# A Fourier-mixing and low-rank MLP kernel: the first batch's turn in rows, U on VectorE, filter blocks shared with ScalarE and GpSimd, stage-1 stores on SyncE, batch 1 inside the MLP

## The chip, the cores and the metric

The kernel runs on one core of a Trainium2 chip. The metric is the device time of one execution in microseconds. The kernel before took 625.9 us (median of three runs, 624.27 to 625.94). The profiled execution of it has a span of 621.1 us.

## The reference

For each of 8 batches of x (3136 tokens, 256 channels, float32) a filter is applied in the frequency domain along the tokens, then a low-rank mix over the tokens, then an MLP over the channels:

```
X = rfft(x, axis=1)                    # 1569 frequencies
y = irfft(X * (filt_r + 1j*filt_i), n=3136, axis=1)
h = (y.T @ U @ V).T                    # U: 3136 x 32, V: 32 x 3136, per batch
u = y + h
out = u + relu(u @ w_ch1) @ w_ch2      # 256 -> 1024 -> 256
```

## The kernel before

**Stages.** 3136 is 64 x 49, so the transforms are matmuls with constant matrices in two factors, in float16.
- Stage 1 (`st1`, L236): for each of the 49 residues r a matmul over 64 tokens (two residues side by side in 128 partitions, the last alone). It gives real and imaginary parts of 32 frequencies, which are evicted to `asb` (`al` for the last) and stored to `ct1` in HBM (L253, L262), a batch in 13 units.
- Stage 2 (`stage2`, L330): reads `ct1` back turned, as blocks `a2` of 98 rows (49 residues, two parts) and 4 x 256 columns (`load_a2`, L301), and transforms along r into a pair of PSUM banks, `pz`. Eight blocks a batch.
- The filter: `pz` times the filter tables. `ta` takes the whole block times `fa`, `tb` its two halves crossed over, times `fc` (L591, L593, L596, on VectorE); GpSimd adds them to `y` (L598).
- Stage 3 (`stage3`, L315): transforms back along r, evicts to `esb` (L309) and stores to `ct2` in HBM (L312).
- `low_rank` (L385): 32 matmuls of `esb` with the transformed U (`uh`) give U's product, evicted as `hp`; a matmul with `kr` (L394) adds up four parts to `h1`.
- Stage 4 (`stage4`, L429): `e2`, 8 residues of `ct2` (L408) with `h1` under them (`put_h`, L414), times `sv`, which holds the last inverse factor above V. The result `ut` is u, turned, for 512 tokens, evicted in two halves (L456 VectorE, L454 ScalarE).
- MLP: `mm1` (L458) is u times a slice of w_ch1, with ReLU on ScalarE into an `h` tile (L465); `mm2_part` (L473) is h times w_ch2 (L494) with u added by a matmul with the identity (L470); the output goes through `och` (L502) to HBM.

**Order.** The order of every engine's instructions is written out by hand: program order is queue order on each engine, and an instruction that waits holds up all behind it in its queue. DMA issues stand in the queue of the engine that starts them (SyncE, ScalarE or GpSimd). The MLP runs over groups of 512 tokens, six a batch, with a group of 128 tokens (the last residue of two batches) after every second batch. A group is eight steps; a step does `mm1` for a slice t of the group and `mm2_part` of the group before it. Work of the next batches is hung on the steps by a planner: `early[s]` runs ahead of step s's `mm1`, `plan[s]` at its end. `plan_mid` (L570) places stages 2 and 3, one VectorE multiply per step, `plan_st1` (L637) the units of stage 1, `plan_rest` (L623) the low-rank part and the loads for stage 4. `ok_dve` (L548) says which steps may take a multiply.

**Batch 0** is done ahead of the MLP and does not go through `ct1`: `u_hat` (L218) transforms U (products L229 on VectorE, sums L233 on GpSimd); `turned` (L271) does stage 1 with x as the weights, so that channels stand in the partitions, and copies the result to `fc` with the rows of one frequency next to each other (L287, L294, L296: elements 98 apart on the write side); `mid_first` (L340) turns four frequencies at a time by transposes (L344, evicted by L347 to `a2`), then does stage 2 into two bank pairs in turn, the filter with doubled matrices (L373 on VectorE, for every third block L368 and L370 on ScalarE and GpSimd) and stage 3. Then come `low_rank`, the loads for stage 4, two stage-4 matmul sets, and all of stage 1 of batch 1, and only then the first step of the MLP. `make_fa` (L562) rewrites the filter tables from batch 0's form to that of the others, in the first four steps.

**Tiles.** [...] mm1 0 and 1, mm2 2 and 3, stage 1 and stage 4 share bank 4, `pz` 5 and 6, stage 3 and low rank 7. `asb` has 2 buffers, `a2` 3, `ta` and `tb` 2, `h` 17. The filters, x, U, V and the weights are loaded by GpSimd's queue; `fb` (the filters) is cleared on VectorE first, and a load into a cleared region waits for that.

Of the kernel before, what the change touches and what calls it, by code (L numbers as in the profile page):

```python
# [13 lines left out]
MULT = mybir.AluOpType.mult  # L14
# [10 lines left out]
def _consts():  # L25
# [30 lines left out]
    w2[1, 1::2, 89:113] = -np.sin(p32)  # L56
    w2s = np.concatenate([w2[:, :, 64:128], w2[:, :, 0:64]], axis=2)
# [43 lines left out]
def kernel(  # L101
# [37 lines left out]
    def bank(tag):  # L139
        of = {"m": (0, 1), "o": (2, 3), "w": (4,), "e": (7,), "f": (0, 1, 2, 3, 4, 7), "e0": (7, 4)}[tag]  # L140
        turn[tag] = turn.get(tag, -1) + 1
        return psum[:, of[turn[tag] % len(of)], :]

# [41 lines left out]
    nc.vector.memset(fb[32:64], 0.0)  # L185
    nc.vector.memset(fb[96:128], 0.0)
    usb = sb.tile([64, NR * RANK], F16, tag="och", bufs=3, name="usb")
# [19 lines left out]
    vnat = sb.tile([128, SEQ], F16, tag="och", bufs=3, name="vnat")  # L207
    nc.gpsimd.dma_start(vnat[64:96, :], moe_V)
# [9 lines left out]
    def u_hat():  # L218
        ud = sb.tile([64, RANK, 2, NR], F16, tag="och", bufs=3, name="ud")
        nc.vector.tensor_copy(ud, free(usb, 0, 64, 0, [[1, RANK], [0, 2], [RANK, NR]]))  # L220
        for p in range(0, RANK, 8):
# [5 lines left out]
            t = [sb.tile([98, NK, 8], F32, tag=tag, bufs=2, name="ut") for tag in ("ta", "tb")]  # L227
# [5 lines left out]
            nc.gpsimd.tensor_add(uh[:, :, p:p + 8], t[0], t[1])  # L233


    def st1(b):  # L236
        for c in range(3):
            asb = sb.tile([128, 8, DM], F16, tag="asb", bufs=2, name="asb")
            for j in range(4):
                pf = bank("w" if b > 1 else "f")  # L240
# [11 lines left out]
            for h in range(2):  # L252
                nc.scalar.dma_start(dram(ct1[b], (24 * h + 8 * c) * 64 * DM,  # L253
                                         [[DM, 64], [64 * DM, 8], [1, DM]]), asb[64 * h:64 * h + 64])
            if b + 1 < NB and c:
                load_x(b + 1, c - 1)
            yield
        pf = bank("w" if b > 1 else "f")
# [3 lines left out]
        nc.scalar.dma_start(dram(ct1[b], 48 * 64 * DM, [[DM, 64], [1, DM]]), al)  # L262
        if b + 1 < NB:
            load_x(b + 1, 2)
            load_x(b + 1, 3)
# [5 lines left out]
    def turned(c):  # L271
        n = 8 if c < 3 else 1
        for hh in range(2):
            for g in range(0, n, 4):
                z = bank("f")
                for i in range(min(n, 4)):
                    if c < 3:
# [4 lines left out]
                    else:  # L282
                        nc.tensor.matmul(z[:, 0:64], xt[0, 3][:, 128 * hh:128 * hh + 128],
# [426 lines left out]
```

## Time and profile before

| | before |
|---|---|
| time, median of 3 | 625.9 us |
| span of the profiled execution | 621.1 us |
| TensorE matmul busy | 514.4 us (83%), 4467 matmuls |
| ScalarE busy | 397.6 us (64%) |
| VectorE busy | 360.9 us (58%) |
| GpSimd busy | 174.0 us (28%) |
| HBM read, written | 57.42 MB, 49.77 MB |
| first matmul of the MLP (L462) | at 98.15 us |
| TensorE busy in 0 to 100 us, by tens | 0.00, 4.69, 0.44, 3.81, 4.49, 8.62, 7.74, 1.90, 6.26, 1.85 |

A group line of the page names line, engine, operation, the tile written and those read, its shape and count; then busy time and mean duration, then the idle time of the engine just before these instructions and what ended it. PE is TensorE's matmul, PEld its weight load, DVE VectorE, ACT ScalarE, POOL GpSimd, SP SyncE; a q after an engine's name is its queue, where a DMA is issued or a wait ends. The chain of waits is followed back from the last instruction, at each step to what released it. The timeline lists instructions by their start, in us from the start of the span. Matmul busy time counts a matmul's whole way through the array, so a busy TensorE is not one at its peak.

### The profile page before, as it was taken

Reading aid. Unit: us, or ns where it says so; the run is one execution under the profiler, and the core shown is the slowest. Engines: PE = TensorE matmul, PEld = TensorE weight load, DVE = VectorE, ACT = ScalarE, POOL = GpSimd, SP = SyncE. Lnnn points to the kernel's source line nnn. Section 1 sums busy time; section 2 is a strip of 40 time slices with the busy share of each in tenths; the row PEclk is TensorE's granted clock in tenths of the full one; section 3 lists DMA queues with packets and bytes.
Section 4 is the critical chain, followed back from the end, with each engine's and each line's share of the span. In section 5 each row is a group of like instructions: output and inputs, shape, how many; then the busy total and the mean of one; then the engine's idle time right before and its main releaser. Section 6 shows DMA issues by size and latency. Waiting matters only on the chain.

```text
span 621.1 us, 11266 instructions
## 1 busy us (share of the span) xinstructions
PE 514.4 (83%) x4467; PEld 376.3 (61%) x4467; DVE 360.9 (58%) x372; ACT 397.6 (64%) x719; POOL 174.0 (28%) x129
## 2 busy tenths in 40 slices
PE   2128545898899889999999889998989889999997
PEld 1124222666567667667767566666767657777775
DVE  7195227777667628773875547764776369832222
ACT  0358515677577656776676658775676757776663
POOL 6814710434133302431231303340422123310000
PEclk9999867999899999999999899999999999999999
DMA  9971485369656584696548775697364454443212
GB/s 214 148 141 38 110 159 154 112 160 239 169 169 166 142 207 126 186 227 165 172 137 222 160 181 153 163 227 194 101 192 142 113 167 137 137 141 111 97 63 98
DMA packets 82597, 95.31 MB, mean 153 GB/s; under 512 B 6853, under 2 KB 63640, under 8 KB 82544
## 3 DMA queue, kind: packets, MB, share of 16 engines
q1 hardware_dynamic: 52000, 67.16, 36.1%
q0 software_dynamic: 7360, 15.91, 15.5%
q10 hardware_dynamic: 23184, 11.53, 7.1%
q8 instruction: 35, 0.57, 0.4%
q14 instruction: 18, 0.15, 0.1%
HBM read 57.42 MB, written 49.77 MB: 173 GB/s over the span
## 4 chain that ended last, share of the span: by engine, by line
PE 58%; DVE 9%; ACT 8%; DMA 8%; ACTq 4%; issue 4%; SPq 1%; POOL 1%; DVEq 0%; POOLq 0%
PE psum L494 21%; PE psum L462 20%; ACTq L253 4%; PE psum L335 4%; DMA a<-ct 4%; PE psum L327 3%; PE psum L448 3%; ACT asb L249 3%; PE psum L470 3%; ACT h L465 2%; DVE tb L596 2%; DVE tb L593 2%; ACT esb L309 2%; PE psum L242 2%; DMA ct<-asb 1%
## 5 line engine op out<-in xcount | busy, mean ns | idle before, releaser
L465 ACT ACTIVATE h<-psum 128x512 f16<-128x512 f32 (+1 forms) x416 | 238.2, 577 | 136.5 <-PE psum L462 110.8
L462 PE MATMUL psum<-ut,w1sb 128*128 128x512 f16 (+1 forms) x832 | 241.9, 374 | 19.1 <-ACT al L261 9.9
L494 PE MATMUL psum<-w2sb,h 128*128 128x256 f16 x1536 | 232.0, 274 | 0.0
L598 POOL TENSOR_TENSOR y<-ta,tb 128x1024 f16<-128x1024 f16 x56 | 118.9, 2122 | 330.1 <-DVE tb L596 294.8
L494 PEld LDWEIGHTS <-h 128*128 128x128 f16 x1536 | 143.8, 98 | 62.2 <-issue 2.6
L462 PEld LDWEIGHTS <-w1sb 128*128 128x128 f16 x832 | 104.5, 145 | 47.3 <-issue 32.5
L502 DVE COPY och<-psum 128x512 f32<-128x512 f32 x96 | 66.2, 689 | 90.8 <-PE psum L470 90.2
L591 DVE TENSOR_TENSOR ta<-psum,fb 128x1024 f16<-128x1024 f32 x56 | 68.6, 1225 | 41.1 <-PE psum L335 37.8
L309 ACT CAST esb<-psum 98x512 f16<-98x512 f32 x128 | 74.9, 590 | 10.4 <-PE psum L327 7.9
L456 DVE CAST ut<-psum 128x512 f16<-128x512 f32 x48 | 35.4, 738 | 74.9 <-PE psum L448 53.9
L593 DVE SCALAR_TENSOR_TENSOR tb<-psum,fc 64x1024 f16<-64x1024 f32 x56 | 68.7, 1226 | 1.4
L596 DVE TENSOR_TENSOR tb<-psum,fc 64x1024 f16<-64x1024 f32 x56 | 68.2, 1218 | 1.0
L335 PE MATMUL psum<-a,w2t 98*128 98x512 f16 x135 | 41.5, 386 | 18.5 <-DVE tb L596 8.3
L448 PEld LDWEIGHTS <-e 96*128 96x128 f16 x768 | 36.2, 99 | 33.7 <-issue 16.2
L249 ACT CAST asb<-psum 128x512 f16<-128x512 f32 x78 | 45.6, 587 | 16.4 <-PE psum L242 8.8
L470 PE MATMUL psum<-idn,ut 128*128 128x128 f16 x392 | 54.2, 220 | 0.0
L448 PE MATMUL psum<-sv,e 96*128 96x64 f16 x768 | 39.2, 195 | 14.1 <-issue 8.2
L327 PE MATMUL psum<-y,g 128*98 128x512 f16 x105 | 39.8, 379 | 6.9 <-ACT esb L309 6.4
L454 ACT CAST ut<-psum 128x512 f16<-128x512 f32 x48 | 35.4, 737 | 9.9 <-PE psum L448 9.9
L470 PEld LDWEIGHTS <-ut 128*128 128x128 f16 x392 | 38.5, 98 | 5.0
L242 PE MATMUL psum<-x,wf 128*128 128x256 f16 x168 | 32.8, 292 | 1.1 <-ACT asb L249 1.1
L296 ACT CAST fc<-psum 128x256 f16<-128x256 f32 x12 | 14.9, 1687 | 21.0 <-PE psum L278 21.0
(76 smaller groups left out, 266.8 us busy)
## 6 DMA issues: line engine op xcount, KB each, us to landing
out_dram<-och SPq DMA_DIRECT2D x48, 512.0 KB
ct<-esb SPq DMA_DIRECT2D x64, 196.0 KB
x<-in_x_dram POOLq DMA_DIRECT2D x24, 512.0 KB, 8.0
e<-ct SPq DMA_DIRECT2D x48, 256.0 KB
a<-ct SPq DMA_DIRECT2D x56, 196.0 KB
ct<-asb ACTq DMA_DIRECT2D x42, 256.0 KB
e<-h SPq DMA_DIRECT2D x24, 128.0 KB
wf<-wf SPq DMA_DIRECT2D x3, 256.0 KB
```

The source lines that it names most:

```text
L309: nc.scalar.copy(esb[b, k][:, 2 * half:2 * half + 2, :].rearrange("p s d -> p (s d)"), pe[0:98])
L335: nc.tensor.matmul(pz, w, a, start=True, stop=True)
L448: nc.tensor.matmul(pu[:, 64 * i:64 * i + 64], e2[b, c][:, i, 128 * dh:128 * dh + 128], sv[:, 64 * r:64 * r + 64], start=(i == 0), stop=Tru ...
L462: nc.tensor.matmul(ph[:, 0:n], w1sb[:, dh, :, t], gr.ut[:, dh, 0:n], start=(dh == 0), stop=(dh == 1))
L465: nc.scalar.activation(h[:, 0:n], ph[:, 0:n], RELU)
L470: nc.tensor.matmul(o[:, dh * 128:dh * 128 + 128], gr.ut[:, dh, t0:t0 + n], idn, start=False, stop=(dh == 1), skip_group_check=True)
L494: nc.tensor.matmul(o, gr.h[tt][:, i * 128:(i + 1) * 128], w2sb[:, tt, :], start=(tt == 0), stop=False, skip_group_check=True)
L502: nc.vector.tensor_copy(gr.och[:, 2 * y:2 * y + 2, :].rearrange("p j d -> p (j d)"), gr.pc)
L591: nc.vector.tensor_mul(ta, pz, va)
L593: nc.vector.scalar_tensor_tensor(out=tb[0:64], in0=pz[64:128], scalar=-1.0, in1=vb, op0=MULT, op1=MULT)
L596: nc.vector.tensor_mul(tb[64:128], pz[0:64], vb)
L598: nc.gpsimd.tensor_add(ys[k], ta, tb)
```

## The change

It is one rewrite with several parts:
- The turn of batch 0: `turned` copies PSUM to `fc` in one piece, 512 elements in a row, and the transposes read columns 32 apart. For this the rows of the stage-2 matrix, and the order of the rows in `ct1`, change.
- `u_hat`: U's copy is divided between VectorE and ScalarE, and the sums go from GpSimd to VectorE. One half of the clearing of `fb` is done by a ScalarE copy from a small cleared tile.
- The middle of batch 0: the evictions of the transposes go from ScalarE to VectorE, and 6 instead of 5 of 16 filter blocks go through ScalarE and GpSimd. x of batch 1 is loaded from inside it.
- The filter blocks of the other batches: two of eight (three in batch 1) are copied out of PSUM by ScalarE, and GpSimd does all their multiplies. The minus sign moves from the multiply into the table (`make_fa`), so that L593 becomes a plain multiply.
- Stage-1 stores are issued by SyncE, not ScalarE, and `asb` has three buffers.
- Stage 1 of batch 1 moves from before the MLP into its steps 3 to 7, three units a step; x of batch 2 is loaded from steps 9 to 15. An empty group of eight half-steps after batch 0 gives batch 1 time to get ready.
- Both halves of `ut` are evicted by VectorE; steps 2 and 6 take no multiply. The second low-rank matmul comes a step later. Three `a2` loads are ahead instead of two, stage 3 comes a step later. U, V and the h tiles share one ring.

```diff
+    order = np.append(np.arange(48).reshape(2, 24).T.reshape(-1), 48)
+    w2 = w2.reshape(2, NR, 2, 128)[:, order].reshape(2, 98, 128)
...
-        of = {..., "e0": (7, 4)}[tag]
+        of = {..., "e0": (7, 4), "w1": (7, 5, 6)}[tag]
...
+    NH = 17
+    hring = cst.tile([128, NH, 512], F16, name="hring")
+    hflat = hring.rearrange("p n f -> p (n f)")
...
-    nc.vector.memset(fb[32:64], 0.0)
+    zero = cst.tile([128, 64], F16, name="zero")
+    nc.vector.memset(zero, 0.0)
     nc.vector.memset(fb[96:128], 0.0)
-    usb = sb.tile([64, NR * RANK], F16, tag="och", bufs=3, name="usb")
+    nc.scalar.copy(fb[32:64].rearrange("p s (k f) -> p (s k) f", f=64),
+                   free(zero, 32, 64, 0, [[0, NK * DM // 64], [1, 64]]))
+    usb = hflat[0:64, 0:NR * RANK]
...
-        nc.vector.tensor_copy(ud, free(usb, 0, 64, 0, [[1, RANK], [0, 2], [RANK, NR]]))
+        for p, eng in ((0, nc.vector.tensor_copy), (16, nc.scalar.copy)):
+            eng(ud[:, p:p + 16], ...)
...
-            nc.gpsimd.tensor_add(uh[:, :, p:p + 8], t[0], t[1])
+            nc.vector.tensor_add(uh[:, :, p:p + 8], t[0], t[1])
...
-            asb = sb.tile([128, 8, DM], F16, tag="asb", bufs=2, name="asb")
+            asb = sb.tile([128, 8, DM], F16, tag="asb", bufs=3, name="asb")
-                pf = bank("w" if b > 1 else "f")
+                pf = bank("w" if b > 1 else "w1")
...
-                nc.scalar.dma_start(dram(ct1[b], (24 * h + 8 * c) * 64 * DM,
-                                         [[DM, 64], [64 * DM, 8], [1, DM]]), asb[64 * h:64 * h + 64])
+                nc.sync.dma_start(dram(ct1[b], (16 * c + h) * 64 * DM,
+                                       [[DM, 64], [128 * DM, 8], [1, DM]]), asb[64 * h:64 * h + 64])
...
-                    dst = free(fc, 0, 128, 3136 * hh + 2 * (24 * h + 8 * c + g),
-                               [[2, 4], [1, 2], [98, 32]])
+                if hh:
+                    nc.vector.tensor_copy(cm[:, o:o + n], z[:, 0:n])
+                else:
+                    nc.scalar.copy(cm[:, o:o + n], z[:, 0:n])
...
-                                        free(fc, 0, 128, 3136 * hh + 98 * (4 * k + i), [[1, 98]]), idn)
-            a2[k] = sb.tile([98, 4 * DM], F16, tag="a2", bufs=3, name="a2")
-            nc.scalar.copy(a2[k], z[0:98])
+                                        free(fc, 0, 128, 3136 * hh + 4 * k + i, [[32, 98]]), idn)
+            a2[k] = sb.tile([98, 4 * DM], F16, tag="a2", bufs=4, name="a2")
+            nc.vector.tensor_copy(a2[k], z[0:98])
...
-            if j % 3 == 2:
+            if j % 5 in (1, 3):
...
+            if j in (4, 6, 8, 10):
+                load_x(1, j // 2 - 2)
...
+        if b == 0:
+            groups.append(Group(None, 7))
...
-        if dh:
-            nc.scalar.copy(o, v)
-        else:
-            nc.vector.tensor_copy(o, v)
+        nc.vector.tensor_copy(o, v)
...
-    for _ in st1(1):
-        pass
...
-        return s % 8 != 2 and not small(s)
+        return s % 8 not in (2, 6) and not small(s)
...
-        nc.vector.tensor_copy(fc[64:128, s], fb[64:128, s])
+        nc.vector.tensor_copy(fc[0:64, s], fb[64:128, s])
+        nc.vector.tensor_scalar_mul(fc[64:128, s], fb[64:128, s], -1.0)
         nc.vector.tensor_copy(fa[64:128, s], fb[0:64, s])
...
-                nc.vector.scalar_tensor_tensor(out=tb[0:64], in0=pz[64:128], scalar=-1.0, in1=vb,
-                                               op0=MULT, op1=MULT)
+                eng.tensor_mul(tb[0:64], p[64:128], vb[64:128])
...
+        def pooled(k):
+            pc = sb.tile([128, 4 * DM], F16, tag="pc", bufs=2, name="pc")
+            nc.scalar.copy(pc, box[k][0])
+            box[k][0] = pc
+            for i in range(3):
+                mul(k, i, nc.gpsimd)
...
+        lead = 5 if b > 1 else 2
+        for k in range(3):
+            at(later(s, -lead), fetch, k)
...
+            if k in on_pool:
+                s = later(s, 1)
+                early[s].append((pooled, (k,)))
+                d = max(later(s, 10), end)
+                s = later(s, 3 if b > 1 else 1)
+            else:
...
+                d = max(later(s, 5), end)
+                s = later(s, 1)
+            at(d, three, k, 0)
+            at(later(d, 1), three, k, 1)
...
+        at(later(s, 2), low_rank_end, b)
...
+    for u in range(13):
+        at(3 + u // 3, step1, 1)
+    for c in range(4):
+        at(9 + 2 * c, load_x, 2, c)
...
-        m = later(start[b - 1], -8) if b > 1 else 5
-        z = plan_mid(b, m, 0 if b == 1 else 3)
+        m = later(start[b - 1], -8) if b > 1 else 10
+        z = plan_mid(b, m, (2, 5) if b > 1 else (1, 3, 5))
```

## The prediction

> **What bounds the kernel now.** I read the busy table by slices first (TensorE fills its slices from about 110 us on, and does little in the first 98), then the chain of waits from 0 to 125 us, the timeline of the first 50 us, and TensorE's waits in the regular part. The chain through the start:
>
> ```profile
> 71.27 2.30 DMA ct<-esb
> ...
> 73.63 3.49 DMA e<-ct
> 77.12 3.73 issue
> 80.85 0.60 PE psum L448 x8
> ...
> 86.12 8.82 DMA ct<-asb
> ...
> 98.15 2.72 PE psum L462 x6
> ```
>
> The first matmul of the MLP (L462) starts at 98.15. Ahead of it stands a round trip through memory (71.27 to 80.85), and then all of batch 1's stage 1 (82.91 to 98.15), most of it one wait of 8.82 us for a store, because only two asb buffers exist. What stands before 71 is in the timeline of the first 50 us (start, length, engine, line; idle time and releaser in brackets):
>
> ```profile
> 27.63 1.44 POOL L233 TENSOR_TENSOR uh<-ut 98x256 f16<-98x256 f32 x2
> 28.43 2.00 DVE L229 TENSOR_TENSOR ut<-psum,tw 98x256 f32<-98x256 f32 x4 [13.14 <-POOL uh L233]
> ...
> 30.18 9.95 ACT L296 CAST fc<-psum 128x256 f16<-128x256 f32 x8 [9.40 <-PE psum L278]
> 30.28 14.74 DVE L294 CAST fc<-psum 128x256 f16<-128x256 f32 x12
> ```
>
> The lines of L229 and L233 are the products and additions of U, L296 and L294 the turned copies of batch 0. VectorE stood 13.14 us because the additions of U (L233) are queued on GpSimd behind all filter loads, which that queue finishes issuing at 27.63. Only then come the turned copies, 14.74 / 12 = 1.23 us each for 256 scattered elements. In the regular part TensorE's waits between 182 and 560 us (us, times, longest) are:
>
> ```profile
> PE psum L462 <- ACT h L465: 8.8, 12, 1.1
> PE psum L335 <- DVE tb L596: 6.8, 8, 1.2
> PE psum L335 <- DMA a<-ct: 6.6, 5, 2.0
> PE psum L327 <- ACT esb L309: 5.2, 3, 1.8
> PE psum L394 <- ACT hp L392: 2.8, 6, 0.5
> ```
>
> That is 30.2 us of 378: TensorE is the bound here, and only these waits can go. The chain around 180 us shows what makes ScalarE late: it issues stores itself.
>
> ```profile
> 179.39 0.59 ACT asb L249
> ...
> 180.01 0.62 ACTq L253
> ...
> 180.66 0.90 ACTq L253
> ```
>
> For 1.5 us no ReLU can run behind an L249, so the next matmul of L462 comes late.
>
> [...] 577 ns for 512 and 1017 for 1024 elements, so 0.86 ns each and 0.14 us fixed. [...] the trace has 2122 ns (L598). [...] the multiply L591 has a minimum, median and maximum of 1224, 1225 and 1225 ns, and GpSimd runs beside some of them. So more GpSimd work shouldn't slow these multiplies. [...] The windows show a granted clock of 0.63 and 0.54 in 80 to 100 us, after the idle stretch; I leave as much of that in the new start.
>
> **U and the turn.** VectorE clears one half of fb instead of two (3.47 us less). The other half goes to ScalarE: 8192 elements x 0.86 + 0.14 = 7.2 us, after its table load (1.28), so from about 2.0 to 9.2. GpSimd's second filter load waits for it, where it waited for VectorE until 9.80 before: no change. The loads of su and tw queue behind it on ScalarE; su leaves at about 9.7 and lands 1.9 us later (the smallest load in the page's list of landings needs that), 11.6. The copy of U in halves (2.78 us before, 1.4 to 1.6 each now) ends at 12.8 on ScalarE. VectorE starts the U products at about 12.5: four rounds of two multiplies (618 ns each) and one addition. The addition isn't in the trace on VectorE; it lies between 0.25 (256 elements at the 0.89 ns of L220) and 0.74 (GpSimd's own), and I take 0.4. That makes 4 x 1.64 = 6.6, to 19.1. The turned copies become six of 128x512 in a row per engine: VectorE 6 x 0.69 (L247) + 0.2 = 4.3, to 23.4; ScalarE 6 x 0.58, hidden beside it. x has landed by 18.1, where the filter issues stop waiting for it. So the transposes start near 23.5 and not 45.47: -22 (-25 to -18). Their weights are read with a stride of 32 elements; w1sb's with a stride of 8 take 145 instead of 98 ns. 64 of these would cost 3 us on a TensorE that isn't this stage's bound: 0 to 2.
>
> **The middle of batch 0** lasts from 45.47 to 71.25, 25.8 us; its busiest engine is ScalarE with 13 x 1.02 + 16 x 0.54 = 21.9. Now VectorE has 10 multiplies x 1.225 and 8 copies of 98x1024 (1.02 to 1.3, I take 1.15) = 21.5, ScalarE 14.8, GpSimd 6 x 2.12. With the same 3.9 us of filling and handing over: 25.4, taken as 26 with the strided weights (24 to 28). It ends near 49.5. The last filter load is issued at 25.34 and lands at 27.2; the last quarter is needed 18 us after 23.5. Hidden. The loads of x for batch 1 stand on GpSimd between its multiplies, half a microsecond each, and have 20 us to land.
>
> **The tail** to the first L462 is 71.25 to 83.05 without stage 1 of batch 1: 11.8. The load of x for batch 2 (at 76.45) no longer runs beside it: 11.4. The MLP starts at 49.5 + 11.4 = 60.9 instead of 98.15: **-37.2**.
>
> **The first groups get it back in part.** VectorE now has 12 x 0.69 = 8.3 us of filter copies (8 before; the negated one is priced like L564), then 6 evictions of stage 1 x 0.69 and two ut copies x 0.74: about 14. Behind them wait stage 1's matmuls, in order with the MLP's, so group 0 takes 14 to 15 instead of 7.3: +7. The last store (2.3 to 3 us) and the a2 load (3.3) follow it, against three steps of slack of 1.2 each: a wait of about 3 where 0.9 and 1.7 were: +0.5. The empty group of eight half-steps splits 7.9 us of MLP into 4.4 of only mm2 and about 6 of only mm1, bound by ScalarE's ReLUs (8 x 0.6): +2. Gone are ScalarE's store issues in the rest of this part (waits of 1.9 and 1.8 at 122 and 134): -3.2. Sum: **+6.3** (+2 to +12).
>
> **The regular part.** Off ScalarE per batch: six ut copies x 0.737 and seven store issues x 0.6; onto it two copies x 1.02. VectorE loses 2 x 3.67 of multiplies and gains 4.4. Both stay under 50 us of a 62 us batch. Waits: L462 8.8 to 2; L394 2.8 to 0 (its matmul comes a step later); L335 on DMA 6.6 to 2 (three loads, ahead of the e loads on SyncE); L335 on VectorE 6.8 to 3 (a pooled block frees its banks after 1.02 instead of 3.67); L327 5.2 to 3. That is -20.2. New: a pooled block needs 1.02 on ScalarE, up to 2.1 behind an addition, and 4 x 2.12 = 8.5 on GpSimd, 11.6 of the 12.5 us that ten steps give; its y may come late, behind it queue stage 3 and the MLP: +3. The stores now stand on SyncE behind output stores and e loads; three asb buffers hide that. The new order of ct1's rows (w2's rows permuted to match) moves the same packets, and U, V and the 17 h tiles in one ring only change place, since U and V are read before the first ReLU writes there: both 0. Sum: **-17.2** (-28 to 0).
>
> 625.9 - 37.2 + 6.3 - 17.2 = 577.8, so **577**.
>
> **Rivals.** (1) The start gains, the regular part does not: each wait of ScalarE comes back as one of SyncE's order or GpSimd's y. For it: the 0.9 us of slack above. Against: GpSimd is busy 28% only. 625.9 - 37.2 + 6.3 = 595. (2) All waits of the regular part go, and the first group overlaps better: -39 + 2 - 28 = 561. Against: the small groups still have too short steps for VectorE. (3) Slower: [...] Then a pooled block needs 12.7 and its wait 3 us more, the next block's addition queues behind, 4 us for each of 15 blocks: +60, and the gain in waits shrinks to 8: 625.9 - 37.2 + 6.3 + 60 - 8 = 647.
>
> **How the numbers follow.** 0.55 for my forecast, 0.22 for (1), 0.16 for (2), 0.06 for (3), 0.01 for no change. The range takes in the bounds of the start (about 6 either way) and reaches to (1) and near to (2): 557 to 600. Faster 0.93, same 0.01, slower 0.06.
>
> **What would show it.** First L344 near 23.5, first L475 near 61 in the new lines; group 0 near 14 us; no ACTq store in the chain; L335 and L475 waits as above. Wrong: U's products starting after 15, a middle of batch 0 over 29, GpSimd multiplies of 64x1024 over 2.2 us, or stage 3 waiting for GpSimd's y in each batch.

## The result, and the profile after

The changed kernel takes **608.98 us** (median of four runs, 601.8 to 610.12) where the kernel before takes 625.92 beside it: a ratio of 0.970, with a 95% interval of 0.961 to 0.978. It is faster, but by 17 us and not by the 48 that were forecast, and 609 lies outside the range of 557 to 600. Its profiled execution has a span of 599.7 us and is the shortest of the four; the other three have spans of 607.0 to 608.1.

I divided both profiled executions into three stretches: up to the first matmul of the MLP (L462, now L471), from there to the first step of the second group of batch 1, and the rest. The last column is the median over the runs of the changed kernel and of its variants in which nothing of that stretch was edited (6, 5 and 8 profiles, this one among them; for the first groups the run with x of batch 2 held back counts too).

| | before | forecast | after, profiled | after, median |
|---|---|---|---|---|
| start, to the first mm1 of the MLP | 98.2 | 60.9 | 65.5 | 66.1 |
| first groups | 81.0 | 87.3 | 101.5 | 102.6 |
| regular part | 441.9 | 424.7 | 432.6 | 437.0 |
| span | 621.1 | 572.9 | 599.7 | 605.7 |

So the start is 5 us worse than forecast, the first groups 15 and the regular part 12, in the typical run. The profile of the kernel before is of an execution of 622.9 us, 3 us under its median, so the last column set against the first shows up to 3 us too little gain. The timeline of the changed kernel's start:

```profile
9.07 2.86 ACT L231 COPY hring<-hring 64x1568 f16<-64x1568 f16 x1
10.00 1.09 DVE L241 TENSOR_TENSOR ut<-psum,tw 98x256 f32<-98x256 f32 x2 [0.96 <-PE psum L236]
11.12 0.42 DVE L245 TENSOR_TENSOR uh<-ut 98x256 f16<-98x256 f32 x1
...
15.82 2.48 DVE L299 CAST fc<-psum 128x512 f16<-128x512 f32 x4
...
52.85 1.74 SPq L418 DMA_DIRECT2D e<-ct  x3
...
54.34 0.61 POOL L165 DMA_DIRECT2D x<-in_x_dram  x1
55.27 2.94 SPq L424 DMA_DIRECT2D e<-h  x3
```

U's products (L241) begin at 10.00 and no longer wait for GpSimd. In the kernel before the first half of them ran at 13.28, as this line of its timeline shows, and the other half only at 28.43:

```profile
13.28 2.01 DVE L229 TENSOR_TENSOR ut<-psum,tw 98x256 f32<-98x256 f32 x4 [0.96 <-PE psum L224]
```

The turned copies (L299) take 0.62 us apiece. The last three lines of the first view are the new tail: three e loads, then a load of x for batch 2 issued right into them, then the puts of h. TensorE's waits in the regular part (167 to 560 us; us, times, longest):

```profile
PE psum L340 <- DMA a<-ct: 10.5, 4, 3.0
PE psum L340 <- DVE tb L600: 4.4, 9, 1.1
PE psum L460 <- DMA a<-ct: 3.1, 1, 3.1
PE psum L332 <- ACT esb L314: 0.9, 3, 0.4
```

The 8.8 us in which mm1 waited for its ReLU and the 2.8 us of the low-rank end are gone from the list, stage 3's 5.2 us are 0.9. The waits for a2 have grown from 6.6 us to 10.5 and 3.1 (the second is a matmul of stage 4, whose wait the profile puts down to the same transfers). The first two groups, in windows (length; busy time and instructions of each engine; granted clock; share of the DMA engines; GB/s):

```profile
core 0: us, PE busy (x) PEld busy (x) DVE busy (x) ACT busy (x) POOL busy (x), PEclk, DMA share, GB/s
65.50:83.60 18.10, 11.31 (x62) 6.38 (x59) 14.53 (x24) 7.38 (x14) 0.95 (x1) 0.71 0.36 70
83.60:100.30 16.70, 11.17 (x80) 7.38 (x80) 6.16 (x8) 5.86 (x11) 1.68 (x1) 0.80 0.50 129
```

They take 34.8 us where the first two took 19.4 before. TensorE waits in both, and once more ahead of batch 1's first group. Its longest waits from 65 to 167 us:

```profile
PE psum L254 <- DVE asb L259: 6.3, 1, 6.3
PE psum L340 <- DMA a<-ct: 5.9, 2, 5.5
PE psum L460 <- DMA e<-h: 5.4, 1, 5.4
```

The first ends at 77.6 (stage 1 of batch 1, for its eviction on VectorE), the second at 92.3 (stage 2, for the a2 data), the third at 151.8 (stage 4 of batch 1, for the put of h). The mean clock of the two groups is 0.71 and 0.80: the trace has it at half (0.50) from 75.9 to 82.7 and from 89.5 to 96.3, and later from 150.9 to 157.8.

### The profile page after: what moved, and what is told of

It is laid out like the page before. It is cut to its first block, busy times and chain, and to the rows that moved or that the text cites. A ratio compares the mean times of both kernels' runs of the same rounds, so it can differ in the third digit from the quotient of the medians.

```text
span 599.7 us, 11562 instructions
## 1 busy us (share of the span) xinstructions
PE 525.0 (88%) x4467; PEld 383.4 (64%) x4467; DVE 332.2 (55%) x384; ACT 379.8 (63%) x676; POOL 266.5 (44%) x171
## 3 DMA queue, kind: packets, MB, share of 16 engines
q0 software_dynamic: 7360, 15.91, 16.3%
## 4 chain that ended last, share of the span: by engine, by line
PE 54%; DVE 8%; ACT 3%; DMA 3%; issue 2%; SPq 2%; DVEq 0%; ACTq 0%
PE psum L471 19%; PE psum L504 19%; PE psum L340 3%; PE psum L460 3%; PE psum L480 3%; PE psum L332 3%; DVE tb L600 2%; DVE tb L598 2%; DMA a<-ct 2%; PE psum L254 2%; DVE och L512 1%; DVE ta L596 1%; PE psum L396 1%; ACT asb L261 1%; SPq L424 1%
## 5 line engine op out<-in xcount | busy, mean ns | idle before, releaser
L475 ACT ACTIVATE hring<-psum 128x512 f16<-128x512 f32 (+1 forms) x416 | 238.2, 576 | 160.7 <-PE psum L471 158.7
L471 PE MATMUL psum<-ut,w1sb 128*128 128x512 f16 (+1 forms) x832 | 243.6, 375 | 0.5 <-DVE ut L465 0.4
L504 PE MATMUL psum<-w2sb,hring 128*128 128x256 f16 x1536 | 233.7, 276 | 0.0
L504 PEld LDWEIGHTS <-hring 128*128 128x128 f16 x1536 | 145.1, 99 | 62.3 <-issue 1.9
L465 DVE CAST ut<-psum 128x512 f16<-128x512 f32 x96 | 71.0, 740 | 150.0 <-PE psum L460 135.5
L471 PEld LDWEIGHTS <-w1sb 128*128 128x128 f16 x832 | 103.2, 145 | 22.7 <-issue 6.2
L596 DVE TENSOR_TENSOR ta<-psum,fb 128x1024 f16<-128x1024 f32 x41 | 50.1, 1221 | 35.3 <-PE psum L340 32.0
L340 PE MATMUL psum<-a,w2t 98*128 98x512 f16 x135 | 43.0, 400 | 22.9 <-DMA a<-ct 16.5
L598 DVE TENSOR_TENSOR tb<-psum,fc 64x1024 f16<-64x1024 f32 x41 | 50.2, 1226 | 1.0
L600 DVE TENSOR_TENSOR tb<-psum,fc 64x1024 f16<-64x1024 f32 x41 | 49.9, 1217 | 0.6
L332 PE MATMUL psum<-y,g 128*98 128x512 f16 x105 | 39.8, 379 | 2.7 <-ACT esb L314 1.5
L340 PEld LDWEIGHTS <-w2t 98*128 98x128 f16 x135 | 13.7, 102 | 31.5 <-issue 26.5
L598 POOL TENSOR_TENSOR tb<-pc,fc 64x1024 f16<-64x1024 f16 x15 | 31.9, 2123 | 1.2
```

The costliest lines, as they stand in the source:

```text
L340: nc.tensor.matmul(pz, w, a, start=True, stop=True)
L465: nc.vector.tensor_copy(o, v)
L471: nc.tensor.matmul(ph[:, 0:n], w1sb[:, dh, :, t], gr.ut[:, dh, 0:n], start=(dh == 0), stop=(dh == 1))
L475: nc.scalar.activation(h[:, 0:n], ph[:, 0:n], RELU)
L504: nc.tensor.matmul(o, gr.h[tt][:, i * 128:(i + 1) * 128], w2sb[:, tt, :], start=(tt == 0), stop=False, skip_group_check=True)
L598: eng.tensor_mul(tb[0:64], p[64:128], vb[64:128])
```

## The experiments

All times are medians, compared with the changed kernel's 609.0 unless another is named; the kernel before took 625.9 to 627.2 beside each of them. Intervals are those of the ratio to the kernel before. Where nothing ahead of the MLP is edited, its first matmul still lies between 65.1 and 69.0 us in six profiles, so a difference of 2 to 3 us in the start of a single profile tells nothing.

### The tail: x of batch 2 held back

```diff
+    def hold():
+        nc.gpsimd.tensor_copy(gate, groups[0].ut[0:1, 1, 510:512])
+    at(9, hold)
     for c in range(4):
         at(9 + 2 * c, load_x, 2, c)
```

> The changed kernel, with the four loads of x(2) held on GpSimd's queue until the second ut copy of group 0 exists (a copy of two elements on GpSimd reads it ahead of them), so that none is issued at 54.3 us. Theory A: the x(2,0) load, 8.35 us on its way beside the e loads and the put of h, is what makes the tail after the middle of batch 0 15.5 us and not 11.4; then e<-h lands 3 to 4.5 us after its issue instead of 6.1, MLP begins at 61 to 63 instead of 65.55, and the kernel takes 2.5 to 4 us less, with no wait on x(2) anywhere. Rival B: e<-h stands behind the e loads, which are alone enough to take that long; then MLP begins within 1 us of 65.5 and the time is the same within 1 us.

603.65 us (0.964, 0.958 to 0.970): 5.3 less. The MLP begins at 62.3; the puts of h land 3.8 to 3.9 us after their issue instead of 6.1 to 7.6. Theory A holds, and the gain is above its 4 us. One of the four x buffers is free by then, and the change took the load out of stage 1, so nothing on GpSimd's queue held it until the tail was over.

### The first groups

Three runs: `make_fa` spread over the groups, `make_fa` in the tail, stage 1 of batch 1 in the tail.

```diff
-        at(i, make_fa, i)
+        at((8, 14, 21, 28)[i], make_fa, i)
```

> The changed kernel, with its four make_fa calls after steps 8, 14, 21 and 28 instead of after steps 0 to 3 (each is first read at step 11, 17, 24 or 31). Theory A: in group 0 the stage-1 evictions of batch 1 on VectorE (L259) stand behind the 10.3 us chain of L570 to L572 from 66.5 to 76.8, which is the 6.5 us gap of TensorE at 77.6 and brings the half-clock stretch with it. Then group 0 falls from 18.1 us to 10 to 12, the L254 wait on L259 from 6.3 us to under 1, and the kernel takes 5 to 9 us less than the changed one (about 601 to 604 median). Rival B: group 0 is held by its 31 stage-1 pieces on TensorE and ScalarE whatever VectorE does, and the wait moves to the a2 fetch of group 1; then group 0 and 1 together stay at 33 to 35 us and the time within 2 us of the changed kernel.

612.79 us (0.977, 0.970 to 0.983): 3.8 more. Group 0 falls to 10.7 us, as theory A says, so the chain of L570 to L572 was what held stage 1's evictions. In group 1 the wait for the a2 data grows from 5.5 to 7.7 us, as rival B had it. And groups 1 to 3 take 19.2, 18.6 and 17.9 us instead of 16.7, 11.3 and 11.4, which neither theory had. VectorE's groups of lines, first of this run from 76 to 135 us (busy time, mean ns, idle time before):

```profile
L572 DVE COPY fb<-fb 64x2048 f16<-64x2048 f16 x4 | 8.0, 2009 | 0.3
L571 DVE TENSOR_SCALAR fc<-fb 64x2048 f16<-64x2048 f16 x4 | 6.7, 1686 | 0.1
L570 DVE COPY fc<-fb 64x2048 f16<-64x2048 f16 x4 | 5.2, 1291 | 0.1
```

and of the changed kernel from 65 to 123 us:

```profile
L571 DVE TENSOR_SCALAR fc<-fb 64x2048 f16<-64x2048 f16 x4 | 2.8, 692 | 0.1
L570 DVE COPY fc<-fb 64x2048 f16<-64x2048 f16 x4 | 2.8, 688 | 0.1
L572 DVE COPY fb<-fb 64x2048 f16<-64x2048 f16 x4 | 2.7, 686 | 0.4
```

The same twelve instructions take 19.9 us where they took 8.3, while GpSimd now multiplies beside them (17.2 of 18.6 us busy in group 2); the next run shows one such copy at 7.37 us beside a GpSimd copy. Behind them the ut copy is late, and stage 1 of batch 2, which shares its bank, waits 10.3 us for it.

```diff
+    for i in range(4):
+        make_fa(i)
+    stage4(groups[0], 0)
```

> The changed kernel, with the four make_fa calls on VectorE between the middle of batch 0 and the first ut copy, where VectorE is idle from 47.6 to 64.4 us, instead of in group 0. Theory A (from the run with make_fa spread): these f16 copies take 0.69 us alone and 1.7 to 2.8 us beside GpSimd's work; in the tail the first three or four run beside the sv copy (2 to 2.8 us), the rest alone, in all 10 to 16 us, so the chain ends between 58 and 64, at most 1 us after what stage 4 waits for. Group 0 falls to 10 to 12 us, group 1 stays at 15 to 19 (its a2 fetch comes no earlier relative to stage 1), and the kernel takes 4 to 8 us less than the changed one. Rival B: the sv copy on GpSimd is slowed by VectorE's copies as much as they by it (6.9 to 10 us or more), stage 4 waits for sv, MLP begins 2 to 4 us later, and the gain is under 4 us.

602.6 us (0.960, 0.953 to 0.968): 6.4 less, theory A. MLP begins at 67.2, group 0 is 10.3 us, group 1 stays at 19.0. The timeline of VectorE and GpSimd in this tail:

```profile
48.36 6.91 POOL L524 COPY sv<-hring 32x3136 f16<-32x3136 f16 x1
48.46 7.37 DVE L568 COPY fc<-fb 64x2048 f16<-64x2048 f16 x1
55.84 0.69 DVE L569 TENSOR_SCALAR fc<-fb 64x2048 f16<-64x2048 f16 x1
```

VectorE's copy, begun 0.1 us after GpSimd's, ends 0.56 us after it, at 55.83; GpSimd's takes 6.91 us, and 6.90 in the changed kernel, where no VectorE copy runs beside it. The expectation had assumed slower copies; here only the first one is long, and the next ones take 0.69 us each. Rival B, that the sv copy is slowed, is refuted.

```diff
+    for _ in st1(1):
+        pass
     stage4(groups[0], 0)
...
-    for u in range(13):
-        at(3 + u // 3, step1, 1)
```

> The changed kernel, with stage 1 of batch 1 issued as a whole between the low-rank products of batch 0 and its first stage 4 (where TensorE is idle from 51.3 to 63.6 us, ScalarE from 51.5) instead of at steps 3 to 7 of group 0: this undoes the part that put batch 1 into MLP. Theory A: it fits into the idle time but for its stores, which share the DMA engines with the e loads and the put of h; MLP begins 0 to 3 us later (65.5 to 68.5), group 0 takes 8.5 to 11 us instead of 18.1 and group 1 10 to 12 instead of 16.7, since the a2 data are long there; the kernel takes 8 to 13 us less. Rival B: the 1.6 MB of stores hold up the put of h and MLP begins 5 us or more later, and groups 2 to 5 inherit the waits; gain under 5 us.

600.43 us (0.960, 0.953 to 0.968): 8.6 less, theory A. MLP begins at 67.9 (2.3 later), group 0 takes 7.2 us. Group 1 takes 15.7 and not 10 to 12: in it mm1 waits 4.5 us for a ut copy that stands behind `make_fa`, which now falls wholly into this time. The first groups last 90.2 us instead of 102.6.

### The middle of batch 0

```diff
-                                        free(fc, 0, 128, 3136 * hh + 4 * k + i, [[32, 98]]), idn)
+                                        free(fc, 0, 128, 3136 * hh + 98 * (4 * k + i), [[1, 98]]), idn)
```

> The changed kernel, with the 64 transposes of batch 0 reading 98 neighbouring columns at 98*(4k+i) instead of 98 columns with a stride of 32; batch 0's input to stage 2 is wrong by this (the columns are in another order), everything else is computed as before. Theory A: the strided weight loads are what made eight transposes take 1.3 to 1.48 us instead of 0.45 to 0.61, and TensorE the bound of batch 0's middle. Then they take 0.45 to 0.65, the middle of batch 0 (20.4 to 49.97, 29.6 us) takes 23 to 26, MLP begins 3 to 6 us earlier, and the kernel takes 3 to 6 us less. Rival B: the middle is bound by the VectorE chain of a2 copies and products, and the transposes wait for their bank; then the eight still take over 1.2 us and the middle stays at 29 to 30.

This kernel leaves out the order of columns that its contiguous copies need, so batch 0's values don't count, only its time. One run: 608.95 us. The transposes of the changed kernel, by source line (minimum, median, maximum in ns, first and last start):

```profile
L349 PEld LDWEIGHTS <-fc x64: 241/261/273, 20.4 to 42.0; 128*98 128x98 f16 x64
L349 PE MATMUL psum<-idn,fc x64: 220/332/428, 20.4 to 42.1; 128*98 128x128 f16 x64
```

and of this run:

```profile
L349 PEld LDWEIGHTS <-fc x64: 120/125/208, 19.8 to 42.1; 128*98 128x98 f16 x64
L349 PE MATMUL psum<-idn,fc x64: 217/220/315, 19.8 to 42.1; 128*98 128x128 f16 x64
```

The stride costs 136 ns a weight load, 8.7 us for 64, and the eight transposes of a block take 0.6 to 1.1 us instead of 1.4 to 1.9: that part of theory A holds. But the middle, from the first transpose to the first low-rank matmul, takes 29.7 us as against 28.9, so its conclusion fails, and so does rival B's, that the transposes would stay slow. TensorE's waits from 20 to 50 us in this run name something else, and GpSimd's timeline shows it:

```profile
PE psum L332 <- POOL uv L375: 5.6, 2, 5.3
```

```profile
29.07 0.55 POOL L220 DMA_DIRECT2D w2sb<-in_moe_w_ch_dram  x1
29.63 4.21 POOL L375 TENSOR_TENSOR uv<-pc,fb 128x1024 f16<-128x1024 f16 x2
```

GpSimd goes on issuing loads until 29.6, and only then comes to its first two products, for which ScalarE's copies have been there since 24.5 and 26.2. The next run, with batch 0's columns out of order in the same way, takes those two away from GpSimd:

```diff
-            if j % 5 in (1, 3):
+            if j in (6, 8, 11, 13):
...
-                uv = sb.tile([128, 2, 2 * DM], F16, tag="ta", bufs=3, name="uv")
+                uv = sb.tile([128, 2, 2 * DM], F16, tag="uv", bufs=5, name="uv")
```

> The run with contiguous transposes (batch 0's data wrong in the order of columns), with GpSimd's products of batch 0 reduced from six to four, j = 6, 8, 11 and 13, so that none stands behind GpSimd's own queue of loads; the two others go to VectorE, with buffers enough for them. Theory A: what kept the middle of batch 0 at 30 us with cheap transposes is that queue, which ends at 28.6 to 29.6, and the two products behind it (to 33.8, with a wait of L332 of 5.3 us); then the middle takes 21 to 25 us (bound by VectorE's 12 products of 1.23 and 8 copies of 0.69 us, 20.3 us in sum), the wait of L332 on L375 falls under 1.5 us, and MLP begins 5 to 8 us earlier than in the changed kernel. Rival B: another bound, such as the filter loads still under way, holds it at 27 us or more.

One run: 606.07 us. The middle takes 23.8 us, the wait of L332 on GpSimd 0.9, as theory A has it; MLP begins at 62.0, 3.5 earlier and not 5 to 8 (the tail is as slow as before). So two bounds of about the same length stood beside each other, TensorE with strided weights and GpSimd's queue, and taking one away leaves the other. That GpSimd's queue is one, these two runs show. That the strided weights are one by themselves rests on the trace: in the changed kernel's middle TensorE stands idle for 1.3 of 28.9 us. No run had strided weights and the two products moved. The last run of these undoes the part with contiguous copies, with the columns of batch 0 in their order:

```diff
+                for h in range(2):
+                    dst = free(fc, 0, 128, 3136 * hh + 4 * (8 * c + g) + 2 * h,
+                               [[4, 4], [1, 2], [98, 32]])
```

> The changed kernel, with batch 0's turn done as in the kernel before: the evictions of stage 1 scatter (1.23 us for 128x256 on either engine, 24 of them and two small ones, where the changed kernel has 14 copies of 0.59 to 0.69 us), and the 64 transposes read 98 neighbouring columns. This undoes the part with contiguous copies and nothing else. Theory A: copies cost 7 to 8 us more before the first transpose (27 to 29 instead of 20.4), the transposes give 6 to 9 us back on TensorE, and by then the queue of loads on GpSimd (to 28.6) no longer stands before its first product, so the middle of batch 0 takes 22 to 25 us; MLP begins within 2.5 us of the changed kernel's 65.5 and the time is within 2 us of it: the contiguous copies bring next to nothing. Rival B: the middle still takes 28 us or more, being bound by VectorE's and GpSimd's products; then 6 to 8 us slower.

612.58 us (0.976, 0.968 to 0.983): 3.6 more. Scattered copies run from 15.8 to 30.6, the first transpose is at 31.0 and not at 20.4, and the middle takes 23.1 us. So the contiguous copies gain 10.6 us and give 5.8 back in the middle. MLP begins at 70.5, 4.9 later. Rival B is refuted; theory A had the middle right and put the end of the copies 2 to 4 us too early, so its conclusion that they bring next to nothing fails.

### The regular part

```diff
-            plan_st1(b, later(start[b - 1], -55))
+            plan_st1(b, later(start[b - 1], -60))
```

> The changed kernel, with stage 1 of batches 3 to 7 begun 60 units of time before the first group of the batch ahead instead of 55. Theory A: at each batch border the first a2 fetch stands in SyncE's queue behind the last stage-1 store and waits for it to land (6.6 us after its issue at 206.5), and stage 2 waits 2 to 3 us for the fetch; with 5 units more (5 to 6 us) the store has landed when the fetch comes up. Then the waits of L340 on a<-ct from batch 3 on fall from about 2.1 to 3.2 us each to under 0.5 and the kernel takes 7 to 11 us less. Rival B: the transfers at the border are bound by the DMA engines (share 1.0 to 1.1 there), so a store issued earlier makes others late; then the waits move to stage 4 or to other borders, and the time falls by 0 to 3 us.

593.05 us (0.946, 0.941 to 0.952): 15.9 less, more than theory A's 11. The groups at the borders of batches 3 to 6, which took 15.3, 13.0, 14.2 and 13.9 us, take 11.9, 11.3, 10.2 and 11.5. It moves stage 1, its x loads and what stands in SyncE's queue together, so it doesn't tell which of them counts.

The clock has a share that theory A left out. In `gate_x2`, where this part of the kernel is as in the changed one, TensorE waits 3.3, 2.8, 3.1 and 3.3 us at the four borders, and just behind the end of each the clock goes to half for 3.4 us (from 218.9, 280.3, 348.6 and 413.5). The changed kernel's own profile, the fastest of its four executions, has two such stretches (348.9 and 413.8). With early stage 1 there is none. The border group of batch 4, first in `gate_x2`, then in this run:

```profile
276.30:290.80 14.50, 11.20 (x83) 7.55 (x82) 7.14 (x8) 5.52 (x10) 2.12 (x1) 0.88 0.70 186
278.80:290.10 11.30, 9.70 (x84) 7.08 (x83) 7.11 (x8) 6.22 (x12) 2.13 (x1) 1.00 0.78 205
```

Four stretches of 3.4 us at half the clock are up to 7 us lost (my estimate), beside the waits' own 12.5.

The border of batch 4 in the changed kernel, as SyncE's timeline and then the chain have it:

```profile
276.73 0.48 SPq L418 DMA_DIRECT2D e<-ct  x1
277.26 0.59 SPq L418 DMA_DIRECT2D e2l<-ct  x1
277.95 0.65 SPq L424 DMA_DIRECT2D e<-h  x1
278.65 0.61 SPq L424 DMA_DIRECT2D e2l<-h  x1
279.30 1.43 SPq L308 DMA_DIRECT2D a<-ct  x3
```

```profile
278.65 0.61 SPq L424
279.30 2.81 DMA a<-ct
282.15 0.59 PE psum L340 x2
```

The a2 fetches stand behind the e loads of the batch ahead, and the first of those waits for the last ct2 store. SyncE's waits of this kind from 182 to 560 us:

```profile
SPq L418 <- DMA ct<-esb: 20.9, 7, 5.0
```

The next run changes only that order:

```diff
-        lead = 5 if b > 1 else 2
+        lead = 9 if b > 1 else 2
```

> The changed kernel, with the first three a2 fetches of batches 2 to 7 planned 9 units ahead of stage 2 instead of 5, stage 1 left at -55. Theory A (queue order): at four of the five borders the fetches stand in SyncE's queue behind the first e load of the batch ahead, which waits 4 to 5 us for the last ct2 store to land; 4 units earlier they are ahead of it. Then the waits at 282, 348 and 413 us go, the groups there fall from 13.0, 14.2 and 13.9 to 10.3 to 11.3, only the border of batch 3 (where the fetch waits 4.3 us for the last stage-1 store itself) keeps its wait, and the kernel takes 6 to 10 us less. Theory B (transfer load): what counts is that the stage-1 stores, the x loads and the ct2 stores are on their way together; then the fetches only wait in place of the e loads, the waits stay at 2 to 3 us or move to stage 4, and the time falls by 0 to 3 us.

601.66 us (0.958, 0.951 to 0.965): 7.3 less, about half of what early stage 1 brings. TensorE's waits from 172 to 560 us in this run, and one of SyncE's from 182 on:

```profile
PE psum L460 <- DMA e<-h: 6.2, 4, 4.5
PE psum L340 <- DVE tb L600: 4.9, 10, 1.1
PE psum L340 <- DMA a<-ct: 3.3, 1, 3.3
```

```profile
SPq L308 <- DMA ct<-al: 17.7, 4, 7.3
```

At the borders of batches 4 to 6 the wait is gone (10.8, 10.7, 10.3 us); one wait for a2 is left, at the border of batch 3, and that one is worse (20.0 us instead of 15.3): there the fetch waits for the last stage-1 store itself, and now the e loads stand behind it. Theory A holds for its three borders, with its reverse side: whichever of the two loads waits, the other is queued behind.

The same edit in the kernel before:

```diff
-                plan_st1(b, later(start[b - 1], -52))
+                plan_st1(b, later(start[b - 1], -57))
```

> The kernel before, with stage 1 of batches 3 to 7 begun at -57 instead of -52, nothing else. Theory A: the border waits (L335 on a<-ct, 6.6 us in five) are there for the same reason and go: 4 to 8 us less than the kernel before. Theory B: in the kernel before ScalarE issues the stage-1 stores and the fetches are two with lead 5 and 4, so the border is not the same; the waits of mm1 on its ReLU stay, and the time falls by 0 to 3 us.

614.17 us (0.979, 0.974 to 0.985): 13 less than the kernel before, more than theory A's 8. Its regular part falls from 441.9 to 430.2. Two of TensorE's waits from 182 to 560 us:

```profile
PE psum L335 <- DMA a<-ct: 3.8, 5, 1.2
PE psum L462 <- ACT h L465: 3.3, 7, 0.8
```

The border waits fall from 6.6 us only to 3.8, which is the smaller part. The waits of mm1 on its ReLU fall from 8.8 to 3.3, which neither theory had, although ScalarE still issues all the stores; and the two stretches at half the clock that the kernel before has in its regular part (from 230.8 and 350.2) are gone. So theory A's size is too small and its mechanism is a part only. The reserve was there all along and isn't the change's doing; and the store issues on ScalarE are not by themselves the cause of the 8.8 us.

The next run gives the issues back to ScalarE:

```diff
-                nc.sync.dma_start(dram(ct1[b], (16 * c + h) * 64 * DM,
+                nc.scalar.dma_start(dram(ct1[b], (16 * c + h) * 64 * DM,
```

> The changed kernel, with all stage-1 stores issued by ScalarE again, as in the kernel before, the rest unchanged. Theory A: the issue on ScalarE was the cause of most of the 8.8 us in which mm1 waited for its ReLU and of part of the residual's waits; those come back and the kernel takes 5 to 12 us more than the changed one, 614 to 621. Rival B: with the stores off SyncE's queue the a2 fetches are no longer queued behind them and the e loads not behind the fetches, so the border waits of 2 to 3 us shrink by as much as ScalarE's issues cost; then within 3 us of the changed kernel, with L471's waits on ScalarE back but L340's on a<-ct under 5 us in all.

615.24 us (0.983, 0.976 to 0.989): 6.3 more, toward the lower end of theory A. Both theories have a share: over the whole run stage 3's wait for ScalarE comes back with 10.8 us and mm1's with 6.5, while L340's on a2 falls from 16.5 to 8.4.

The last of these leaves the filter blocks of batches 2 to 7 on VectorE:

```diff
-        z = plan_mid(b, m, (2, 5) if b > 1 else (1, 3, 5))
+        z = plan_mid(b, m, () if b > 1 else (1, 3, 5))
```

> The changed kernel, with no filter block of batches 2 to 7 given to ScalarE and GpSimd (batch 1 keeps its three): this undoes that part of the change. Theory A: two blocks in a batch are 7.3 us of VectorE work, and with them VectorE has 4 more waits a batch of the kind L340 on L600 (1.1 us); the planner's middle gets two to four steps longer, so e is loaded later for the next batch: 4 to 10 us slower than the changed kernel. Rival B: VectorE is busy 53% in these stretches and off the path that sets the end, the waits at the borders are the transfers'; within 2 us of the changed kernel, or faster by up to 4, as GpSimd's late products (2.13 us each) go too.

606.04 us (0.966, 0.959 to 0.974), with overlapping runs: no slower, perhaps 3 faster. The regular part is 435.7 us as against 437.0. Theory A is refuted: the filter blocks on ScalarE and GpSimd bring nothing. Nor does the planner's middle get longer, as theory A had it: worked out from the kernel's planner, it ends at the same steps with and without them (for batch 3 at step 144).

### Together

Stage 1 of batch 1 in the tail, x of batch 2 held, stage 1 at -60; then also:

```diff
-        at(i, make_fa, i)
+        at((0, 2, 6, 9)[i], make_fa, i)
...
-            if n + 1 < len(groups) and t in (2, 6) and groups[n + 1].c < 7:
-                stage4(groups[n + 1], t // 4)
+            if n + 1 < len(groups) and t in ((2, 6) if n != 6 else (6, 7)) and groups[n + 1].c < 7:
+                stage4(groups[n + 1], t // 4 if n != 6 else t - 6)
```

> Stage 1 of batch 1 in the tail, the loads of x(2) held until the second ut copy, and stage 1 of batches 3 to 7 begun at -60 instead of -55, all three in the changed kernel. Theory A: the three gains lie in different stretches and add: 5.3 (x(2) held, measured) and 15.9 (early stage 1, measured) and 8 to 13 (stage 1 in the tail), so 575 to 580 us median. Rival B: x(2) held frees the DMA engines for a put of h that the stage-1 stores then take again, so the first gain vanishes: 580 to 585; and if stage 1 in the tail brings nothing, 588 or more.

577.01 us (0.920, 0.915 to 0.926): the gains add. That it is the figure once forecast for the changed kernel is chance.

> Stage 1 of batch 1 in the tail, x(2) held, early stage 1, and two more edits: make_fa after steps 0, 2, 6 and 9, each behind the ut copy of its step and all before GpSimd's first product (84.8), and stage 4 of batch 1's first group at steps 6 and 7 of the empty group instead of 2 and 6. Theory A: the 4.5 us in group 1 in which mm1 waits for a ut copy behind make_fa's chain goes, and the 5.3 us wait of stage 4 on the put of h is filled by the second matmuls of the group before: 7 to 9 us less than with the first three alone, 568 to 570 us median. Rival B: the first wait only moves to the a2 fetch, which is no earlier, and the second to the start of batch 1's first group: 574 to 577.

**568.47 us** (0.908, 0.902 to 0.915), theory A, and the fastest of all. The first groups take 82.8 us and the regular part 418.6, with no stretch at half the clock in it. The wait of stage 4 for the put of h falls from 5.4 to 3.1 us. The second of the two edits restores something: the kernel before already had stage 4 of batch 1's first group at steps 6 and 7 of the group ahead (its `n != 5`), and the change put it at 2 and 6 without naming it as a part. TensorE's waits from 148 to 560 us:

```profile
PE psum L340 <- DVE tb L602: 5.1, 10, 1.1
PE psum L460 <- DMA e<-h: 1.7, 1, 1.7
PE psum L332 <- ACT esb L314: 1.1, 3, 0.4
PE psum L340 <- DMA a<-ct: 0.9, 1, 0.9
```

> The fastest version so far (stage 1 of batch 1 in the tail, x(2) held, early stage 1, make_fa spread behind the ut copies, stage 4 late in the empty group) with all filter blocks of batches 2 to 7 on VectorE. Theory A: with the border waits gone, a group with stage 2 in it is bound by TensorE's own work (10.3 us), VectorE has room, and giving blocks to ScalarE and GpSimd brings nothing here either: within 2.5 us of that version. Theory B: VectorE's blocks are then the longest chain and the middle ends later, so e comes later at each border: 4 us or more slower.

571.67 us (0.912, 0.907 to 0.916). The median is 3.2 us higher, a little outside theory A's 2.5, but the two intervals overlap, the regular part is 418.8 us as against 418.6, and the starts of the two profiles, where nothing differs, are 61.6 and 65.3. The blocks on ScalarE and GpSimd are worth nothing here either, as far as this can be told.

## Why the prediction was wrong, by its own steps

**The direction was right, and the parts that were priced as work came out.** U's products begin at 10.0, against 12.5: su and tw were issued at 0.94 and 1.51, before ScalarE's clearing copy and not behind it, which gave more than the slower U copy (2.86 us against 1.4 to 1.6) took. ScalarE's clearing copy took 7.02 us (7.2; the 577 ns for 512 elements are the page's mean over two sizes of ReLU, and copies of 512 have medians of 585 and 586). The addition on VectorE is 0.42 (0.4), the turned copies 0.62, the first transpose at 20.4 against 23.5. The a2 copies of 98x1024 take 0.69 us, below the bounds of 1.02 to 1.3. GpSimd's 64x1024 multiplies take 2.12 us and not twice that, with which the third rival's 12.7 us were reckoned, so it was empty. In the regular part three of five waits fell as much as forecast or more (mm1's, the low-rank one, stage 3's), that of L335 on VectorE from 6.8 to 4.4 and not to 3, and the 3 us for a late y of GpSimd were not needed.

**The middle of batch 0: "TensorE isn't this stage's bound", 26 us.** It took 29.6 by the end used there (49.97 against 49.5). The weights were priced from a stride of 8 as 0 to 2 us; they cost 8.7, and TensorE, idle for only 1.3 us of the middle, had become a bound. The other bound had no term: GpSimd's queue of loads, seen to end at 27.63 in before, was moved from 18 us ahead of the middle to 8 us into it; the prediction asked whether the filters land in time, not when GpSimd gets to its first product. The early start of 3.1 us was used up here.

**The tail: 11.4 us "without the x load".** It took 15.6. The step took away the x(2) load where it stood before and didn't ask what would now stop it from being issued earlier: nothing. With the load held, the puts of h land in 3.8 us and the time from the first low-rank matmul to mm1 falls from 16.3 to 12.5.

**The first groups: +6.3, measured +20.5, and +21.6 in the median.** The term "group 0 takes 14 to 15" was right in its mechanism, VectorE's queue, and 3.6 us too small; "a wait of about 3" for the a2 data was 5.5; the last group of batch 0 with the empty group behind it, 24.8 us where that last group took 15.2 before, held a further wait of 5.4 for the put of h, which no term had. What no term priced either is the clock: around the end of each of the three waits (6.3, 5.5 and 5.4 us) the clock is at half for 6.8 us. Some 15 us of the three stretches lie behind the end of the wait (77.6 to 82.7, 92.3 to 96.3, 151.8 to 157.8), in which TensorE is busy, so that 7 to 8 us are lost (my estimate, half of these 15) in addition to the waits' own 17.2. The prediction reckoned with a lower clock for the start alone. In the trace the clock falls 4.6, 2.7 and 4.5 us after TensorE stops. But at the borders of the same profile it fell behind a shorter wait too (2.76 us, ended at 348.29) and did not behind a longer one (2.99 us, ended at 282.15), so the length of one wait doesn't decide it. With stage 1 back in the tail, where TensorE is idle anyway, the first groups last 90.2, and 82.8 with `make_fa` behind the ut copies: the part that was to hide batch 1 inside the MLP moved work out of an idle stretch into a full one.

**The regular part: -17.2, measured -9.3, and -4.9 in the median.** The step that failed is "L335 on DMA 6.6 to 2 (three loads, ahead of the e loads on SyncE)". They are not ahead: the planner puts the fetches of batch 4 at step 147 and the first e load of batch 3 at step 144 (in the kernel before at 139 and 138), since the middle of the batch ahead ends there. This could have been worked out from the planner's own numbers. So these waits went to 10.5 and 3.1 us and not to 2. `lead_9` shows that the order is worth 7.3 us; early stage 1, which moves the stores too, gets the forecast 424.7 us and more (419.7). How its other 8 to 9 us divide between stores that land in time and a clock that stays up, no run separates.

**The chances.** The first rival, "the start gains, the regular part does not", at 595, had the right kind of failure, and the range reached to 600. What it missed is that three misses came together. Most of them are of one kind: a wait that takes the place of the one removed, in a queue the change had made earlier or longer. The strided weights, mis-sized, are not.

## What to carry to other kernels

When a stage is moved up, list for each engine what stands in its queue at the new time, DMA issues too, and ask of each load what now keeps it from starting too early. Before work is hidden inside a busy loop, look whether the idle stretch it leaves was hiding it already. Where two loads share a queue and each waits for its own store, the order of the two is a bound of its own; give both stores time to land rather than swap them.

## What the runs showed of the hardware

- VectorE's f16 copy of 64x2048 from SBUF takes 0.69 us alone (the changed kernel, L570). Begun 0.1 us after a GpSimd copy of 6.91 us it took 7.37 (`fa_tail`, once), and GpSimd's was not slowed. Among GpSimd's multiplies `make_fa`'s twelve instructions took 19.9 us (`spread_fa`), without them 8.3: here its place counts more than its length. The multiplies that read PSUM, for which the prediction had asked this, show nothing of the kind: in the changed kernel VectorE's L598 takes 1225 to 1226 ns in all 41 cases, and GpSimd is busy for 11.1 of the 11.3 us of group 2.
- A weight load of 98 columns with a stride of 32 f16 elements takes 261 ns (the changed kernel, L349), with neighbouring columns 125 (`t_contig`).
- A VectorE copy of 98x1024 f16 from PSUM takes 0.69 us (the changed kernel, L352); 128x512 from float32 takes as long (L299, 686 ns).
- The stretches at half the clock seen here are 6.8 us long around waits of 5.4 to 6.3 us in the changed kernel, and 3.4 us behind waits of 2.8 to 3.3 us at the borders in `gate_x2`; the changed kernel's wait of 2.99 us has none. Eight matmuls of L504 take 1.89 us in such a stretch (from 152.21 in the changed kernel) and 1.04 outside (from 145.30). So the waits with a stretch cost more than their own length.
